# Turning v to channel-major by DMA transposes instead of TensorE matmuls, from the second group on

## The chip, the cores and the metric

The kernel runs on one core of a Trainium2 chip. The metric is device time in microseconds (us), the median of the runs named with it. A ratio is the mean time of one kernel's fast runs over that of the other kernel's fast runs of the same rounds, so it is not quite the ratio of the medians quoted. Faster or slower takes 2%. Spans in the profiles are about 2 us shorter than device times.

## The reference

```python
B, N, C = (4, 6080, 256)                 # q, k, v: float32
qn = q / (norm(q, axis=1) + 1e-06);  kn = k / (norm(k, axis=1) + 1e-06)
s = kn.transpose(0, 2, 1) @ qn / tau     # 256 x 256 for each of 4 batches
a = softmax(s)
x = (v @ a).reshape(24320, 256)
h = x @ w_in                             # 256 -> 2048
g = s * relu(h) ** 2 + b
out = g @ w_out                          # 2048 -> 256
```

## The kernel before

The kernel never forms `v @ a`: it folds the softmax into the first weight (`wa`) and computes `h` from v itself. For this v must lie with channels on the partitions (`vT`), while it arrives with rows on the partitions, so each block of v is transposed; the text calls this the turn of v. The rows are cut into 48 groups of 512 (the last has 256), each group into 16 steps. A step is two matmuls into `h_ps` (L417), ReLU on Scalar, a square on Vector, and, four to five steps later, four matmuls into `o_ps` (L441). At the end of a group Vector copies `o_ps` out of PSUM into `o_sb` (the eviction) and adds `rowconst`, a row made once from sums over w_out. Side work (loads, turns of v, the Gram matrix of the next batch) is hung on steps.

```python
def load_v(g):                      # GpSimd queue, float32 to fp16
    ...
    v16 = vpool.tile([P, TG // P, C], FP16, tag="v16", name="v16")      # 4 buffers
    po(nc.gpsimd.dma_start(out=v16[:, :nj, :], in_=...))

def transpose_v(g):
    _, nj = group(g)
    v16 = v_tiles.pop(g)
    vT_ps = ps_h.tile([P, CH, TG], FP16, tag="h_ps", name="vT_ps")
    for j in range(nj):
        for ch in range(CH):
            po(nc.tensor.transpose(vT_ps[:, ch, ts(j, P)], v16[:, j, ts(ch, P)], ident16))   # L272
    vT = vtpool.tile([P, CH, TG], FP16, tag="vT", name="vT")            # 3 buffers
    po(nc.vector.tensor_copy(out=vT[:, :, : nj * P], in_=vT_ps[:, :, : nj * P]))             # L274
    vT_tiles[g] = vT
...
for c in range(len(g0.chunks)):     # start: all q and k of batch 0, then
    g0.load(c)
# w_in, v of group 0, w_out in two halves, v of groups 1 and 2, in this order on GpSimd's queue
...
at_step((g - 3) * FT + 2, lambda g=g: load_v(g))          # g >= 3, FT = 16 steps
at_step((g - 1) * FT + 4, lambda g=g: transpose_v(g))     # g >= 1; used from step 16 g on
```

## Time and profile before

Device time before is 783.38 us (783.3 to 783.8, three runs).

| | busy us | share of the span |
|---|---|---|
| TensorE (PE) | 753.2 | 96% |
| Scalar (ACT) | 517.8 | 66% |
| Vector (DVE) | 505.2 | 65% |
| GpSimd (POOL) | 57.2 | 7% |

The prediction below shows the page's chain and the groups concerned. A row of a group reads: line, engine, operation, output and input, count, then busy us and mean ns, then idle time of the engine before it and what ended that.

### The profile page before, as it was taken

To read this page: it belongs to the slowest core of one execution; us is meant where nothing else is said; L and a number is where in the kernel's file an instruction comes from. 1 tells how busy PE (TensorE), PEld (TensorE's weight loads), DVE (VectorE), ACT (ScalarE), POOL (GpSimd) and SP (SyncE) were. 2 spreads that over 40 slices of the span, in tenths; PEclk is the share of its full clock that TensorE was granted. 3 is DMA by queue.
4 is the path that set the end of the run, shared out by engine and by line. 5 is a ranking of instruction groups with operands and counts; after the bars stand their busy time and mean duration, and the time that the engine had idled before them with its cause. 6 is when DMAs were issued, how large, how long until landed. Compare 5 with 4: busy or idle time off the path is not lost.

```text
span 781.2 us, 14420 instructions
## 1 busy us (share of the span) xinstructions
PE 753.2 (96%) x5646; PEld 527.4 (68%) x5646; DVE 505.2 (65%) x1106; ACT 517.8 (66%) x858; POOL 57.2 (7%) x111
## 2 busy tenths in 40 slices
PE   2689999999999999999999999999999999999997
PEld 2456777767677777776667667776667766666666
DVE  3767676676656766666566666766566565565565
ACT  3466666666766666766766666666676666666665
POOL 3410010001000010000001000000000000000000
PEclk9689999999999999999999999999999999999999
DMA  8999425115535164124715645131113113121011
GB/s 158 212 263 186 96 44 130 41 41 101 131 76 115 41 133 95 41 42 85 145 41 96 129 85 108 46 75 45 41 48 74 42 42 83 42 52 51 28 55 42
DMA packets 22421, 66.34 MB, mean 85 GB/s; under 512 B 2752, under 2 KB 3328, under 8 KB 22352
## 3 DMA queue, kind: packets, MB, share of 16 engines
q0 software_dynamic: 15152, 40.51, 29.4%
q1 hardware_dynamic: 7200, 24.91, 9.8%
q8 instruction: 44, 0.72, 0.4%
q14 instruction: 25, 0.20, 0.1%
HBM read 78.91 MB, written 24.90 MB: 133 GB/s over the span
## 4 chain that ended last, share of the span: by engine, by line
PE 93%; DMA 5%; issue 1%; ACT 1%; DVE 0%; POOL 0%; POOLq 0%
PE o_ps L441 42%; PE h_ps L417 42%; PE s_ps L120 4%; DMA qc<-in_q_dram 4%; PE vT_ps L272 3%; PE wa_ps L237 2%; DMA v<-in_v_dram 1%; ACT r L420 0%; PE n_ps L185 0%; ACT eT L214 0%; PE t_ps L208 0%; ACT L214 0%; DVE o_sb L449 0%; PE rc_ps L338 0%; POOL kc L108 0%
## 5 line engine op out<-in xcount | busy, mean ns | idle before, releaser
L420 ACT ACTIVATE r<-h_ps 128x512 f16<-128x512 f32 (+1 forms) x768 | 450.0, 593 | 225.8 <-PE h_ps L417 199.9
L427 DVE TENSOR_TENSOR g<-r 128x512 f16<-128x512 f16 (+1 forms) x768 | 321.9, 420 | 243.4 <-ACT r L420 236.6
L441 PE MATMUL o_ps<-w_out,g 128*128 128x256 f16 x3040 | 456.8, 273 | 0.0
L417 PE MATMUL h_ps<-vT,wa 128*128 128x512 f16 (+7 forms) x1632 | 453.0, 364 | 0.6 <-ACT r L420 0.6
L441 PEld LDWEIGHTS <-g 128*128 128x128 f16 x3040 | 295.2, 98 | 183.0 <-DVE g L427 0.2
L417 PEld LDWEIGHTS <-wa 128*128 128x128 f16 x1632 | 157.9, 98 | 30.0 <-issue 0.8
L120 PE MATMUL s_ps<-qc,kc 128*128 128x256 f16 (+1 forms) x384 | 72.9, 296 | 18.5 <-DMA qc<-in_q_dram 18.5
L449 DVE SCALAR_TENSOR_TENSOR o_sb<-o_ps,s_out,rowconst 128x512 f32<-128x512 f32 x95 | 71.1, 748 | 6.4 <-PE o_ps L441 5.6
L261 POOL DMA_DIRECT2D v<-in_v_dram x48 | 25.7, 535 | 617.0 <-PE vT_ps L272 597.6
L143 ACT ACTIVATE sq<-kc 128x1024 f16<-128x1024 f16 (+3 forms) x49 | 50.0, 1031 | 21.9 <-DMA kc<-in_k_dram 18.7
L120 PEld LDWEIGHTS <-kc 128*128 128x128 f16 (+1 forms) x384 | 40.2, 106 | 26.8 <-issue 10.2
L140 DVE TENSOR_TENSOR sq<-qc 128x1024 f16<-128x1024 f16 (+3 forms) x49 | 32.6, 675 | 11.1 <-DMA qc<-in_q_dram 11.1
L274 DVE COPY vT<-vT_ps 128x1024 f16<-128x1024 f16 (+1 forms) x48 | 32.5, 677 | 4.3 <-PE vT_ps L272 4.3
L156 DVE TENSOR_TENSOR f<-sq 128x1024 f16<-128x1024 f16 (+1 forms) x47 | 31.8, 685 | 0.3
L272 PE MATMUL vT_ps<-ident,v 128*128 128x128 f16 x380 | 29.5, 221 | 2.0 <-DMA v<-in_v_dram 2.0
L272 PEld LDWEIGHTS <-v 128*128 128x128 f16 x380 | 25.5, 99 | 3.5 <-DMA v<-in_v_dram 2.4
L156 DVE TENSOR_TENSOR f<-f 128x512 f16<-128x512 f16 (+3 forms) x47 | 25.8, 550 | 0.4
L237 PE MATMUL wa_ps<-w_in,eT 128*128 128x512 f16 x64 | 18.9, 398 | 0.0
L242 ACT ACTIVATE wa<-wa_ps,rs 128x512 f16<-128x512 f32 x16 | 11.0, 687 | 7.6 <-PE wa_ps L237 4.3
L108 POOL DMA_DIRECT2D qc<-in_q_dram x26 | 14.2, 548 | 13.7 <-DMA qc<-in_q_dram 7.7
L108 POOL DMA_DIRECT2D kc<-in_k_dram x26 | 14.2, 548 | 11.4 <-DMA kc<-in_k_dram 9.1
L244 DVE TENSOR_SCALAR wa<-wa_ps,rs 128x512 f16<-128x512 f32 x16 | 11.9, 745 | 1.4 <-PE wa_ps L237 1.2
(37 smaller groups left out, 55.9 us busy)
## 6 DMA issues: line engine op xcount, KB each, us to landing
out_dram<-o_sb SPq DMA_DIRECT2D x47, 512.0 KB, 3.7
v<-in_v_dram POOLq DMA_DIRECT2D x47, 256.0 KB, 5.1
kc<-in_k_dram POOLq DMA_DIRECT2D x20, 512.0 KB, 8.1
qc<-in_q_dram POOLq DMA_DIRECT2D x20, 512.0 KB, 10.0
w_out<-in_moe_w_out_dram POOLq DMA_DIRECT2D x2, 1024.0 KB, 13.2
kc<-in_k_dram POOLq DMA_DIRECT2D x3, 480.0 KB, 8.4
qc<-in_q_dram POOLq DMA_DIRECT2D x3, 480.0 KB, 10.3
w_in<-in_moe_w_in_dram POOLq DMA_DIRECT2D x1, 1024.0 KB, 12.5
```

Source lines behind the costliest of these rows:

```text
L120: po(nc.tensor.matmul(self.s_ps[:, ch, :], kc[:np_, j, ts(ch, P)], qc[:np_, j, :], start=(c == 0 and j == 0 and ch == 0), stop=(c == len(s ...
L140: po(nc.vector.tensor_mul(st["sq"][:np_, 0, js, :], qc[:np_, js, :], qc[:np_, js, :]))
L143: po(nc.scalar.activation(out=st["sq"][:np_, 1, js, :], in_=kc[:np_, js, :], func=AF.Square))
L156: po(nc.vector.tensor_add(st["f", half][:np_, arrays], src[:np_, arrays, :half, :], src[:np_, arrays, half : 2 * half, :]))
L237: po(nc.tensor.matmul(wa_ps, st["e"][:, j, ts(m, P)], w_in16[:, j, ds(fo * NW, NW)], start=(j == 0), stop=(j == CH - 1)))
L272: po(nc.tensor.transpose(vT_ps[:, ch, ts(j, P)], v16[:, j, ts(ch, P)], ident16))
L274: po(nc.vector.tensor_copy(out=vT[:, :, : nj * P], in_=vT_ps[:, :, : nj * P]))
L417: po(nc.tensor.matmul(dst, wa[:, ci, ts(m, P)], src, start=(ci == 0), stop=(ci == CH - 1), skip_group_check=True))
L420: po(nc.scalar.activation(out=r16[:, :n], in_=h_ps[:, :n], func=AF.Relu))
L427: po(nc.vector.tensor_mul(g16[:, :n], r16[:, :n], r16[:, :n]))
L441: po(nc.tensor.matmul(o_halves[g, h][:, j % 2, :], g16[:, ts(j, P)], w_out16[:, m, :], start=(m == 0 and j == js[0]), stop=(m == FT - 1 an ...
L449: po(nc.vector.scalar_tensor_tensor(out=o_sb[:, js[0] : js[-1] + 1, :], in0=o_halves.pop((g, h)), scalar=s_out, op0=ALU.mult, in1=rowconst ...
```

## The change

The intent is to take the turn of v off TensorE, which bounds the kernel. From group 1 on, four DMA transposes per group on the SP queue take the place of eight matmuls and a copy. (The DMA's transposing path is called the crossbar below.) They are placed early (26 steps ahead of use, except for groups 1 and 2 at the start), the loads of v a group earlier, and v and vT get one more buffer each.

```diff
-    vpool = ctx.enter_context(tc.tile_pool(name="vpool", bufs=4))
-    vtpool = ctx.enter_context(tc.tile_pool(name="vtpool", bufs=3))
+    vpool = ctx.enter_context(tc.tile_pool(name="vpool", bufs=5))
+    vtpool = ctx.enter_context(tc.tile_pool(name="vtpool", bufs=4))
...
+    def crossbar_v(g):
+        _, nj = group(g)
+        v16 = v_tiles.pop(g)
+        vT = vtpool.tile([P, CH, TG], FP16, tag="vT", name="vT")
+        for j in range(nj):
+            po(nc.sync.dma_start_transpose(out=vT[:, :, ts(j, P)], in_=v16[:, j, :]))
+        vT_tiles[g] = vT
...
         if g >= 3:
-            at_step((g - 3) * FT + 2, lambda g=g: load_v(g))
+            at_step(max(g - 4, 0) * FT + 2, lambda g=g: load_v(g))
         if g >= 1:
-            at_step((g - 1) * FT + 4, lambda g=g: transpose_v(g))
+            at_step(max((g - 2) * FT, 4 * (g - 1)) + 6, lambda g=g: crossbar_v(g))
```

## The prediction

> **What bounds the kernel now.** I read the page first (busy shares, then the chain that ended last, then the groups), next the waits, next the timeline around one turn of v, and last the start-up. The busy shares and the chain:
>
> ```profile
> PE 753.2 (96%) x5646; PEld 527.4 (68%) x5646; DVE 505.2 (65%) x1106; ACT 517.8 (66%) x858; POOL 57.2 (7%) x111
> ...
> PE 93%; DMA 5%; issue 1%; ACT 1%; DVE 0%; POOL 0%; POOLq 0%
> PE o_ps L441 42%; PE h_ps L417 42%; PE s_ps L120 4%; DMA qc<-in_q_dram 4%; PE vT_ps L272 3%; PE wa_ps L237 2%; DMA v<-in_v_dram 1%; ACT r L420 0%; PE n_ps L185 0%; ACT eT L214 0%; PE t_ps L208 0%; ACT L214 0%; DVE o_sb L449 0%; PE rc_ps L338 0%; POOL kc L108 0%
> ```
>
> A busy share of 96% alone proves little, since matmuls overlap in the records. The chain is the stronger view: 93% of the span is TensorE work that nothing but the matmul before it releases, and the turn of v (vT_ps, L272) is 3% of the span inside that chain. Vector, Scalar and GpSimd together carry about 1%. So TensorE's own stream of rows sets the end, and the turn of v lies in it. The groups concerned:
>
> ```profile
> L274 DVE COPY vT<-vT_ps 128x1024 f16<-128x1024 f16 (+1 forms) x48 | 32.5, 677 | 4.3 <-PE vT_ps L272 4.3
> ...
> L272 PE MATMUL vT_ps<-ident,v 128*128 128x128 f16 x380 | 29.5, 221 | 2.0 <-DMA v<-in_v_dram 2.0
> ```
>
> The mean of 221 ns is not what a turn costs the path, because eight of them run pipelined. The cost is the distance between the starts on either side, in the timeline of TensorE:
>
> ```profile
> 410.94 0.60 PE L417 MATMUL h_ps<-vT,wa 128*128 128x384 f16 x4
> 411.38 0.60 PE L441 MATMUL o_ps<-w_out,g 128*128 128x256 f16 x4
> 411.81 0.60 PE L417 MATMUL h_ps<-vT,wa 128*128 128x384 f16 x4
> 412.25 0.60 PE L441 MATMUL o_ps<-w_out,g 128*128 128x256 f16 x4
> 412.69 0.61 PE L272 MATMUL vT_ps<-ident,v 128*128 128x128 f16 x8
> 413.13 0.60 PE L417 MATMUL h_ps<-vT,wa 128*128 128x384 f16 x4
> ```
>
> A step without the turn is 411.81 - 410.94 = 0.87 us; the step with it is 413.13 - 411.81 = 1.32 us. The difference, 0.44 to 0.45 us, is the distance from 412.69 to 413.13: eight turns at 55 ns. I read the same 0.44 to 0.45 us at 256, 600, 614, 700 and 715 us. There is no gap on either side, so the copy on Vector costs TensorE nothing: vT is made twelve steps before it is used.
>
> **What the Trainium skill says.** (1) "TensorE: Matmul & The Clock Gate", Part 4, gives about 390 ns for one 128x128 turn alone and about 275 ns in one kernel. The trace disagrees for the cost on the path: 55 ns. I use the trace. (2) "VectorE: DVE Perf Modes", The three transpose paths, gives 1309 ns for one 128x128 turn by the DMA crossbar. No run here shows it yet; I use it as the pessimistic rate. (3) "DMA: Bandwidth & Descriptors", Issuing engines are not separate DMA queues: transfers from all issuers run on the same 16 engines and interleave. The trace before has no transpose on any queue, so it cannot show how one shares them. (4) "Perfetto Trace Analysis", Identifying Dependency Chains, says that an instruction with several waits may have extra semaphore instructions put ahead of it; below I say what the trace shows of their cost.
>
> **The change part by part.**
>
> Removed from TensorE: the turn of groups 1 to 47. L272 ran 380 times; group 0 keeps its eight, so 372 go: 46 full groups of eight and a last one of four. 46 x 0.44 us = 20.2 us, and the last, at 758.08 to 758.30, 0.22 us. Together 20.5 us, all of it on the path: 783.4 - 20.5 = 762.9 us.
>
> Removed from Vector: 47 copies out of PSUM, 47 x 0.68 = 32 us of its 505 busy. Off the path: it makes 0 us. The same for the PSUM buffer that vT_ps took from the pool of four: in the whole trace TensorE waited 0.6 us for Scalar to free one.
>
> Added: four transposes per group on the SP queue, each 128x256 fp16, so two 128x128 blocks and 64 KB. 46 x 4 + 2 = 186 of them, 12 MB in all. Per group at the pessimistic 1.31 us per block, one after another: 8 x 1.31 = 10.5 us (an estimate from the skill's figure). A group lasts about (781 - 47) / 47.5 = 15.5 us now, 15.0 us later, so even that rate keeps up. The SP queue otherwise issues one store of the output per group, 0.33 to 0.35 us of issue (at 67.42 and 413.67). The DMA engines are busy 36 to 47% of 100 to 500 us and 13 to 24% after, and there the transposes have room.
>
> Moved: the transposes of group g are placed at step 16(g-2)+6, behind the store of group g-3 at step 16(g-2)+4, and are needed at step 16g. That is 26 steps x 0.87 = 22.6 us of lead for 10.5 us of work. The loads of v are placed a group earlier and v has a fifth buffer; GpSimd no longer waits for TensorE to turn a group but for the SP queue's transposes to have read it:
>
> ```profile
> POOL v L261 <- PE vT_ps L272: 597.6, 42, 16.0
> ```
>
> Those 597.6 us are GpSimd standing before its next load: idle time of an engine that issues transfers, worth nothing by itself. It says that v buffers pace all its loads, those of q and k behind them too. After the change buffers come free earlier, and all loads run further ahead.
>
> **The tight place is group 1**, which has the least lead:
>
> ```profile
> 34.18 1.12 POOL L261 DMA_DIRECT2D v<-in_v_dram  x2
> ...
> 49.96 0.61 PE L272 MATMUL vT_ps<-ident,v 128*128 128x128 f16 x8
> ...
> 60.04 0.59 PE L417 MATMUL h_ps<-vT,wa 128*128 128x512 f16 x2
> ```
>
> The load of v for group 1 is the first of the pair at 34.18, behind w_out. In the slices of 30 to 70 us the rate is near 410 GB/s from 41 to 46 us, which I take for w_out (no change of type, so twice the rate); v for group 1 then lands near 47.5 us (256 KB at 215 GB/s is 1.2 us after it; my inference). Counting steps of 0.87 us, group 1 is first used at the matmul of 60.04 us. So there are 12 us for an estimated 10.5 us, while the loads already fill the 16 engines. It should just do; if other loads get in between, TensorE waits once for some microseconds. Group 2 follows to about 69 us and is needed after 75. I allow 1 us on average for group 1, which makes 763.8 us.
>
> **The rivals.**
>
> A wait at each group start. The first matmul of a group waits for four transfers instead of one copy, so for several semaphores. Three extra instructions of 50 ns would be 0.15 us x 47 = 7 us and leave 770 us. Against it: L120 waits for two DMA tiles (kc and qc), and its two matmuls at 414.88 are followed by the next at 415.10, just their own 0.22 us. TensorE's queue hides such waits once the data is there. I give it one in ten.
>
> The DMA becomes the bound. If a transpose took a multiple of 1.31 us per block, or held up the loads of q and k beside it, each group would wait for vT: at double the rate, 21 us of transposes per 15 us group, the span would pass 1000 us. The engines' free share and the long lead speak against it; that the trace has no transpose in it leaves it possible. One in twenty-five.
>
> Only the start suffers. Between 36 and 68 us the engines are full. If packets of the transposes alternate with loads and each waits its turn, group 1 could come 5 to 10 us late: 768 to 773 us, within 2%. One in six.
>
> The gain is hidden anyway. If another engine were close behind TensorE, taking 20 us away would only uncover it. Against it: Scalar at 66% and Vector at 65%; per step of 0.87 us Scalar needs 0.60 and Vector 0.42 for the main work, with idle before each. I see nothing that takes over.
>
> **Range and chances.** The centre is 762.9 + 1 = 763.8 us, 2.5% less. The low end, 761.5 us, is the full gain and a little from the freed Vector at the start. The high end, 770 us, is group 1 late by 7 us or a small wait per group. Faster by over 2% means under 767.7 us, 4.8 us above the bare sum: 0.74. Within 2%: 0.22. Slower by over 2%: 0.04.
>
> **What would show it.** Right: vT_ps stands at eight matmuls in all; the step that had the turn lasts 0.87 us; TensorE's idle time from 100 us on stays near nothing; the waits show no vT, or one wait by the first matmul of group 1; the loads of v no longer wait for vT_ps. Wrong: L417 waits for the DMA of vT at every group start, the issue-to-landing time of a transpose exceeds the lead of 22 us, the span between 47 and 110 us is longer than before, or the first matmul of each group starts late although its data has landed. The prediction falls most easily on the transfer time of a transpose under load, which no view of the kernel before contains.

## More of the kernel before

The queue of GpSimd carries all loads, the hardware queue the stores:

```profile
q0 software_dynamic: 15152, 40.51, 29.4%
q1 hardware_dynamic: 7200, 24.91, 9.8%
```

## The result, and the profile after

The changed kernel took 770.05 us (769.07 to 770.35, four runs) against 783.59 us of the kernel before on the same chip; ratio 0.9825, 95% interval 0.9808 to 0.9842. That is 13.5 us less, but within 2%, and 6.3 us above the predicted centre.

From the page after: the busy shares, the chain, and the queues:

```profile
PE 734.9 (96%) x5274; PEld 507.1 (66%) x5274; DVE 479.4 (62%) x1059; ACT 517.7 (67%) x858; POOL 57.3 (7%) x111
...
PE 90%; DMA 7%; issue 1%; ACT 1%; SPq 0%; POOL 0%; DVE 0%; POOLq 0%
...
q0 software_dynamic: 15152, 40.51, 28.5%
q1 hardware_dynamic: 60768, 37.12, 18.1%
...
vT<-v SPq DMA_TRANSPOSE x186, 2.4
```

TensorE has 372 matmuls fewer (5646 - 5274) and is busy 18.3 us less. But the chain now has 7% of DMA where it had 5%, and one of its pieces is new: the transfer of vT, 2%. The hardware queue has 53,568 packets more for 12.2 MB more: 288 packets for each of 186 transposes, mostly of 256 bytes.

**Where did the time go?** The start of Vector's first eviction of each group (`o_sb`, L449 before, L458 after) is a clock that both traces have:

| end of group | before, us | after, us | after is ahead by |
|---|---|---|---|
| 0 | 65.55 | 72.71 | -7.16 |
| 1 | 81.42 | 88.14 | -6.72 |
| 2 | 97.56 | 103.82 | -6.26 |
| 10 | 224.20 | 227.05 | -2.85 |
| 20 | 379.67 | 378.05 | 1.62 |
| 46 | 770.46 | 757.77 | 12.69 |
| 47 | 777.11 | 764.42 | 12.69 |

From group 0 to group 46 the changed kernel gains 19.85 us in 46 groups, 0.43 us a group (0.29 to 0.45 in every full group when the traces are read group by group): the predicted gain, in full. All that is missing was lost before 72.71 us. In the timeline of TensorE after (start, duration, line and work, and in brackets the idle time before it and what ended that):

```profile
60.40 0.60 PE L450 MATMUL o_ps<-w_out,g 128*128 128x256 f16 x4
65.99 1.01 PE L426 MATMUL h_ps<-vT,wa 128*128 128x512 f16 x2 [4.99 <-DMA vT<-v]
66.80 1.06 PE L450 MATMUL o_ps<-w_out,g 128*128 128x256 f16 x4
...
70.21 1.06 PE L426 MATMUL h_ps<-vT,wa 128*128 128x512 f16 x2
71.06 0.74 PE L450 MATMUL o_ps<-w_out,g 128*128 128x256 f16 x4
...
71.86 0.59 PE L426 MATMUL h_ps<-vT,wa 128*128 128x512 f16 x2
72.29 0.60 PE L450 MATMUL o_ps<-w_out,g 128*128 128x256 f16 x4
```

TensorE stands idle for 4.99 us before the first matmul of group 1. Then the same four matmuls take 1.06 us where they took 0.60 before the wait. The stretches of time show why. Their columns are the length, then busy time of TensorE, its weight loads, Vector, Scalar and GpSimd (with counts), the granted TensorE clock, the DMA share and GB/s; after:

```profile
60.00:63.00 3.00, 1.00 (x8) 0.46 (x5) 3.00 (x7) 0.96 (x2) 0.00 (x0) 1.00 1.10 195
63.00:66.00 3.00, 0.01 (x1) 0.04 (x2) 0.46 (x2) 0.00 (x0) 0.00 (x0) 0.75 1.51 123
66.00:68.00 2.00, 2.00 (x7) 1.25 (x8) 0.33 (x1) 0.60 (x1) 1.59 (x4) 0.50 0.32 48
68.00:70.00 2.00, 2.00 (x8) 0.91 (x6) 0.58 (x2) 0.40 (x1) 1.59 (x4) 0.50 1.05 186
70.00:72.00 2.00, 2.00 (x11) 1.23 (x10) 0.49 (x2) 0.80 (x2) 0.00 (x0) 0.66 1.07 211
72.00:75.00 3.00, 3.00 (x23) 2.06 (x21) 2.53 (x5) 1.75 (x4) 0.00 (x0) 1.00 1.04 206
```

The third number from the right is the clock: 0.75, 0.50, 0.50, 0.66, then 1.00 again. In the kernel before it is 1.00 throughout these stretches. The Trainium skill, "TensorE: Matmul & The Clock Gate", Part 1, says that an idle window of about 3.4 us takes the clock to half, and that as long a stretch of work brings it back. The fall agrees here: TensorE was idle from 61.00 us, and the clock was at 0.50 from about 64.5 us, 3.5 us later. The return took longer than the page's figure: work began again at 65.99 us and the clock was back at about 71.3 us, 5.3 us later.

**Why was group 1 late?** Its transposes were issued from 48.89 us on, 1.25 us each, so issue was over by 54. But the transfers hardly moved. The queues between 54 and 56 us (packets, MB, share of 16 engines), after:

```profile
q0 software_dynamic: 102, 0.40, 97.3%
q1 hardware_dynamic: 100, 0.03, 9.5%
```

and between 64 and 66 us, when the loads had run out:

```profile
q1 hardware_dynamic: 932, 0.21, 142.4%
q0 software_dynamic: 3, 0.00, 1.1%
```

102 packets of loads, 100 packets of transposes: one for one. A packet of a load there is 0.40 MB / 102 = 3.9 KB, one of a transpose about 256 bytes. By the shares of time, a packet of a load held its engine for 0.973 x 2 us x 16 / 102 = 0.31 us, one of a transpose for 0.03 us: taking turns one for one, the transposes got a tenth of the time. The skill has the rule, which the prediction had only as a rival ("If packets of the transposes alternate with loads"): "DMA: Bandwidth & Descriptors", Queues, rings and completion order, says that each engine goes round the queues it has work for, packet by packet. Group 1 is 4 x 288 = 1152 packets; at 100 in 2 us they would need 23 us, for which there were 12. The other stretches from 54 to 62 us read the same (176 and 178, 100 and 99, 102 and 100).

The loss adds up. The first matmul of group 0 starts at 48.91 instead of 47.58 us: 1.33. Of this, 0.46 us is that v of group 0 landed later (L272 at 42.56 against 42.10 us), and 0.86 us that the matmuls of `wa` after it (L237) took 5.53 instead of 4.67 us, on a clock that came back later (experiments 9 and 10). The transposes can't be the cause, since the first was issued at 48.89 us. The wait: 4.99. From the first matmul of group 1 to the end of group 0: 6.72 instead of 5.51 us (65.55 - 60.04 before), 1.21; this holds the cold clock, less a wait of 1.17 us for rowconst that the kernel before had here and that is now over in time (its profile names Scalar, but Vector's last sum for rowconst ended at 62.14 us and the matmul started at 62.24). Together 7.5 us; the table says 7.16 + 0.44 for the turn of group 1 that fell away, 7.6. Group 1 itself is 4.99 + 1.21 = 6.2 us of it.

### The profile page after: what moved, and what is told of

Its sections match the earlier page's. It is cut to its first block, busy times and chain, and to the rows that moved or that the text cites. A ratio compares the mean times of both kernels' runs of the same rounds, so it can differ in the third digit from the quotient of the medians.

```text
span 768.4 us, 14012 instructions
## 1 busy us (share of the span) xinstructions
PE 734.9 (96%) x5274; PEld 507.1 (66%) x5274; DVE 479.4 (62%) x1059; ACT 517.7 (67%) x858; POOL 57.3 (7%) x111
## 2 busy tenths in 40 slices
DMA packets 75988, 78.52 MB, mean 102 GB/s; under 512 B 56320, under 2 KB 56896, under 8 KB 75920
## 4 chain that ended last, share of the span: by engine, by line
PE 90%; DMA 7%; issue 1%; ACT 1%; SPq 0%; POOL 0%; DVE 0%; POOLq 0%
PE o_ps L450 42%; PE h_ps L426 42%; PE s_ps L120 4%; DMA qc<-in_q_dram 4%; DMA v<-in_v_dram 2%; DMA vT<-v 2%; PE wa_ps L237 1%; SPq L283 0%; PE n_ps L185 0%; ACT r L429 0%; ACT eT L214 0%; PE t_ps L208 0%; POOL kc L108 0%; POOL w_out L295 0%; PE rc_ps L347 0%
## 5 line engine op out<-in xcount | busy, mean ns | idle before, releaser
L426 PEld LDWEIGHTS <-wa 128*128 128x128 f16 x1632 | 159.6, 98 | 36.2 <-issue 6.3
L120 PE MATMUL s_ps<-qc,kc 128*128 128x256 f16 (+1 forms) x384 | 71.8, 291 | 19.3 <-DMA qc<-in_q_dram 19.2
L458 DVE SCALAR_TENSOR_TENSOR o_sb<-o_ps,s_out,rowconst 128x512 f32<-128x512 f32 x95 | 71.1, 749 | 6.5 <-PE o_ps L450 5.7
L237 PE MATMUL wa_ps<-w_in,eT 128*128 128x512 f16 x64 | 19.8, 415 | 0.0
L237 PEld LDWEIGHTS <-eT 128*128 128x128 f16 x64 | 6.6, 105 | 3.7 <-issue 2.5
L343 DVE TENSOR_TENSOR w_out<-w_out 128x512 f32<-128x512 f32 (+1 forms) x8 | 5.2, 651 | 0.0
```

Of the source, the lines that this page charges most:

```text
L120: po(nc.tensor.matmul(self.s_ps[:, ch, :], kc[:np_, j, ts(ch, P)], qc[:np_, j, :], start=(c == 0 and j == 0 and ch == 0), stop=(c == len(s ...
L237: po(nc.tensor.matmul(wa_ps, st["e"][:, j, ts(m, P)], w_in16[:, j, ds(fo * NW, NW)], start=(j == 0), stop=(j == CH - 1)))
L426: po(nc.tensor.matmul(dst, wa[:, ci, ts(m, P)], src, start=(ci == 0), stop=(ci == CH - 1), skip_group_check=True))
L458: po(nc.vector.scalar_tensor_tensor(out=o_sb[:, js[0] : js[-1] + 1, :], in0=o_halves.pop((g, h)), scalar=s_out, op0=ALU.mult, in1=rowconst ...
```

## The experiments

All changes are to the changed kernel unless said otherwise. Runs of one job share the runs of the kernel before (783.44 us in the first job, 784.12 in the second, 783.98 in the third).

**1. Group 1 back on TensorE.**

```diff
-        if g >= 1:
+        if g == 1:
+            at_step(4, lambda: transpose_v(1))
+        if g >= 2:
```

> Only group 1 goes back to TensorE, at its old place (step 4); groups 2 to 47 stay on the crossbar. Theory (the loss is one late start: 5.0 us of wait for group 1 and a cold TensorE clock for some 5 us after it): the wait by L426 on the transposes is gone, the clock stays at 1.00 between 60 and 75 us, and the time is 762.9 + 0.44 for group 1 = 763.3 us, up to 764.7 if the 1.3 us later start of the first matmul stays. Rival (the loss is spread: a cost at each group start, or other transfers held up by transposes): at most 0.5 us better than the changed kernel, so about 769.5 us.

Measured: 764.5 us (763.88 to 764.85), ratio 0.9755. No wait for vT is left in the trace, and the clock is 1.00 from 60 to 75 us:

```profile
63.00:66.00 3.00, 2.62 (x17) 1.86 (x18) 1.52 (x4) 1.19 (x2) 0.00 (x0) 1.00 1.11 188
66.00:68.00 2.00, 2.00 (x16) 1.37 (x14) 1.73 (x4) 1.19 (x2) 0.00 (x0) 1.00 1.07 207
```

So one group of 47 cost 5.5 us. The rival of a loss spread over the groups falls. This kernel is still 1.15 us behind the kernel before at the end of group 0; experiment 9 is about that.

**2. Loads and buffers alone.** All turns back on TensorE at their old steps; fifth v buffer, fourth vT buffer and early loads stay.

```diff
-            at_step(max((g - 2) * FT, 4 * (g - 1)) + 6, lambda g=g: crossbar_v(g))
+            at_step((g - 1) * FT + 4, lambda g=g: transpose_v(g))
```

> All turns back on TensorE with their copies, at their old steps; only the fifth v buffer, the fourth vT buffer and the earlier loads of v are kept. Theory (buffers and early loads are worth nothing by themselves): 783.5 us, within 0.5 us of before. Rival (the earlier loads of v, which come ahead of q and k at the start, delay the first matmul): about 1.3 us more than before, 784.9 us.

Measured: 783.77 us, ratio 1.0004 (0.9988 to 1.0021). The loads and buffers by themselves do nothing, good or bad; and the first matmul is not delayed by them (0.09 us ahead of before at the end of group 0).

**3. One transpose per group instead of four.**

```diff
-        for j in range(nj):
-            po(nc.sync.dma_start_transpose(out=vT[:, :, ts(j, P)], in_=v16[:, j, :]))
+        po(nc.sync.dma_start_transpose(
+            out=vT[:, :nj].rearrange("p j c q -> p (j c) q"),
+            in_=v16[:, :nj, :].rearrange("p j c -> p (j c)")))
```

> One transpose of 128x1024 per group instead of four of 128x256; vT is laid out with the block number outside. Theory A (each transpose costs a fixed price for setup and completion, so four of them are slow beside full loads): group 1 lands several microseconds earlier, the 5.0 us wait goes to under 2 us, about 764 to 767 us. Theory B (the price is per 256-byte packet: the changed kernel added 288 packets a transpose, and each waits its turn among the packets of the loads): the packets are as many, group 1 is as late, 769 to 771 us.

Measured: 770.01 us, ratio 0.9827; TensorE waits 4.7 us for group 1 as before. Between 54 and 56 us the queues show 101 packets of loads and 101 of transposes. Theory A falls, and the counts fit theory B: the price is per packet, and one instruction of 256 KB has nearly as many packets as four of 64 KB.

**4. A quiet start.** The loads that compete with group 1 are held on GpSimd until step 9, and the next batch's first stage starts later so that its loads are not missed.

```diff
+    def hold_pool():
+        po(nc.gpsimd.tensor_copy(out=gate, in_=g16s[9][:, 0:1]))
+    at_step(9, hold_pool)
+    at_step(9, lambda: load_v(2))             # was loaded before the first step
-            at_step(max(g - 4, 0) * FT + 2, lambda g=g: load_v(g))
+            at_step(max((g - 4) * FT + 2, 9), lambda g=g: load_v(g))
-        w0 = first_group[b - 1] * FT + (18 if b == 1 else 6)
+        w0 = first_group[b - 1] * FT + (40 if b == 1 else 6)
-            at_step(max(3, sc - 16), ...gr.load(c))
+            at_step(max(10, sc - 16), ...gr.load(c))
```

> All of groups 1 to 47 on the crossbar as in the changed kernel, but the loads of v from group 2 on and those of the next batch's q and k are held on GpSimd until step 9 (about 57 us), and that batch's first stage starts 22 steps later; so the engines carry nothing else while group 1 is transposed. Theory (the transposes of group 1 are slow only because loads fill the 16 engines): four issues of about 1.24 us, landing by about 57 us, no wait for group 1, 763 to 765 us unless the held loads come late themselves. Rival (the first transposes are slow by themselves, or the wait comes from the late landing of v): the wait of 4 to 5 us stays, 769 to 771 us.

Measured: 766.11 us, ratio 0.9778. Between 48 and 54 us the four transposes of group 1 land 2.4 us after their issue, where they took 13.2 us in the changed kernel in the same stretch. First this kernel, then the changed one:

```profile
q1 hardware_dynamic: 864, 0.20, 16.8%
q0 software_dynamic: 15, 0.02, 1.6%
...
vT<-v SPq DMA_TRANSPOSE x4, 2.4
```

```profile
q0 software_dynamic: 526, 1.26, 108.6%
q1 hardware_dynamic: 76, 0.02, 2.3%
...
vT<-v SPq DMA_TRANSPOSE x4, 13.2
```

Group 1 is in time. The held loads themselves then made a later group late by 2.25 us (at 79.10 us, the transposes landing 10 to 13 us after issue among the loads released), which accounts for the time above the 765 us expected. It is the same mechanism at another place: the loads, not the crossbar by itself and not the issue, set the landing.

**5. The old buffers.** On top of experiment 1: four v buffers, three vT buffers, loads of v at their old steps.

```diff
-    vpool ... bufs=5            ->   bufs=4
-    vtpool ... bufs=4           ->   bufs=3
-            at_step(max(g - 4, 0) * FT + 2, lambda g=g: load_v(g))
+            at_step((g - 3) * FT + 2, lambda g=g: load_v(g))
```

> The kernel with group 1 on TensorE (764.5 us), with the buffers and loads of v of the kernel before: four v buffers, three vT buffers, loads a group later. Theory (the late group 1 came from the full engines at the start, and later groups have 22 us of lead): no wait for vT appears, 764.5 us within 0.7. Rival (the crossbar's longer hold on the v buffers is what the fifth buffer pays for): loads of v come late, transposes of some groups land after their step, waits by L428 on vT, over 766 us.

Measured: 764.17 us (763.03 to 765.14), ratio 0.9742; no wait for vT. The fifth buffer and the early loads are not needed.

**6. Twice as many transposes.** On top of experiment 1, every group from 8 on is transposed a second time into a tile that nobody reads.

```diff
+        if g >= 8:
+            vX = vtpool.tile([P, CH, TG], FP16, tag="vX", name="vX")
+            for j in range(nj):
+                po(nc.sync.dma_start_transpose(out=vX[:, :, ts(j, P)], in_=v16[:, j, :]))
```

> The kernel with group 1 on TensorE (764.5 us), and every group from 8 on is transposed a second time into a tile that nothing reads: 158 more transposes. Theory (in the steady state the transposes are hidden wholly and do not slow TensorE): 764.5 us within 0.7; SP then issues for some 10 us of the 14 us of a group. Rival (transposes cost TensorE or the loads something each): double that cost, at least 1 us slower; if the second set makes SP or the crossbar the bound, waits by L428 on vT.

Measured: 764.83 us, ratio 0.9752 against 0.9755 of experiment 1. The DMA share from 100 to 400 us rises from 0.45 in experiment 1 to 0.61, the median landing over the whole run from 2.4 to 3.5 us, and TensorE sees nothing of it. In the steady state the transposes are hidden, with room for as many again.

**7. Keeping the clock up during the wait.** Group 1 is late as in the changed kernel, but 16 matmuls into an unused PSUM tile stand where TensorE would be idle.

```diff
+        if s == FT:
+            warm_ps = ps_h.tile([P, TG], FP32, tag="h_ps", name="warm_ps")
+            for _ in range(16):
+                po(nc.tensor.matmul(warm_ps, w_in16[:, 0, :P], w_in16[:, 0, :TG], ...))
```

> The changed kernel (group 1 still late) with 16 matmuls of 128x512 into an unused PSUM tile just before the first matmul of group 1, where TensorE stands idle for 5.0 us: 3.5 us of work that nobody needs. Theory (the wait is paid twice, by its own 5 us and by some 2.4 us more at half clock after it): the clock stays at 1.00 from 60 to 72 us and the time falls by 1.5 to 2.5 us to about 767.5 to 768.5 us. Rival (only the wait counts; the slow steps after it have another cause): 770 us, no change.

Measured: 767.0 us (766.85 to 767.79), ratio 0.9783, half a microsecond better than the best that was expected. The clock is 1.00 from 60 to 75 us. Its timeline:

```profile
60.44 3.62 PE L420 MATMUL warm_ps<-w_in 128*128 128x512 f16 x16
65.40 0.59 PE L431 MATMUL h_ps<-vT,wa 128*128 128x512 f16 x2 [1.35 <-DMA vT<-v]
65.83 0.60 PE L455 MATMUL o_ps<-w_out,g 128*128 128x256 f16 x4
```

The data come as late as ever, yet useless work in the gap makes the kernel 3 us faster: the steps after the wait run at full speed. At the end of group 0 it is 3.2 us ahead of the changed kernel; 0.6 of that is that its transposes landed sooner (65.40 against 65.99 us), so the cold clock is worth some 2.6 us, a little more than expected.

**8. More lead for group 1.** The load of v for group 1 goes ahead of the two loads of w_out.

```diff
     load_v(0)
+    load_v(1)
     w_out_rows = ...
     ...
-    load_v(1)
     load_v(2)
```

> The changed kernel with the load of v for group 1 moved ahead of the two loads of w_out. Theory (group 1 only lacks lead: it took 17 us beside full loads and had 12): v for group 1 lands some 5 us sooner, near 43.8 us, its transposes land near 60.5 us or sooner, the wait is 0 to 1 us, the clock stays up, and the time is 763.5 to 765 us; w_out lands 1.2 us later, which may cost up to 0.5 us. Rival (the transposes end when the loads let up, whenever they start): they land near 65 us again, 769 to 770 us.

Measured: 770.75 us, ratio 0.9827, no better. The transposes were issued 5.1 us earlier (from 43.76 us), and group 1 was used later still:

```profile
66.97 1.01 PE L426 MATMUL h_ps<-vT,wa 128*128 128x512 f16 x2 [5.45 <-DMA vT<-v]
```

My theory missed here and the rival fits: as long as the loads fill the engines, an earlier issue gains little. From 48 to 62 us the packets alternate again (109 and 109, 104 and 103 in two of the 2 us stretches). The packet count alone would have had group 1 through near 63 us; the traces show what held its last transfer. The last load then under way, of q, was issued at 49.51 us and landed 17.1 us later, at 66.6; the last transpose of group 1, issued at 47.65, landed 19.2 us later, at 66.8. In the changed kernel the two landed at 65.2 (49.40 + 15.8) and 65.9 us (52.78 + 13.1). So in both the transposes end just after the loads do. The loads end because no new ones come: GpSimd's next load of v waits for these transposes to free a buffer (17.4 us here, 16.5 in the changed kernel). Why that load of q ended 1.4 us later here is open.

**9 and 10. Keeping the clock up before the first group.** 48 matmuls of 128x128 on a tile of ones, while TensorE waits for the load of v for group 0; once on top of experiment 1, once in the kernel before.

```diff
+    warm_ps = ps_h.tile([P, P], FP32, tag="h_ps", name="warm_ps")
+    for _ in range(48):
+        po(nc.tensor.matmul(warm_ps, ones16, ones16, start=True, stop=True, ...))
     transpose_v(0)
```

> The kernel with group 1 on TensorE (764.5 and 764.2 us in two jobs) with 48 matmuls of 128x128 on a tile of ones, which nobody reads, between 39.8 and 42.5 us, where TensorE waits for the load of v for group 0. Theory (what is still missing against the bare sum, 1.15 to 1.5 us at the end of group 0, is a TensorE clock that stays at half from 42 to some 47 us, while in the kernel before it came up at some 45 us): the clock is 1.00 from 42 us on or soon after, the first matmul of group 0 starts 1 to 2 us sooner than 48.8 us, and the time is 762 to 763.3 us. Rival (the later start comes from loads that land later): no change, 764.2 to 764.5 us.

> The kernel before with the same 48 matmuls at the same place. Theory: there the clock comes up at about 45 us, so the gain is smaller, 0.5 to 1.2 us, about 782.5 us. Rival (no effect of the clock): 783.5 us.

Measured: 762.4 us (ratio 0.9732, the fastest of all) and 783.18 us (ratio 0.9993, interval 0.9979 to 1.0007). Of the four runs on top of experiment 1 three took 762.01 to 762.46 and the profiled one 764.31; in that one the clock had gone to 0.51 between 40 and 42 us in spite of the matmuls, and its mean over the run was 0.991, against 0.996 to 0.998 in the three. In the profile of the kernel before with them the clock stays at 1.00 from 36 to 50 us, and it is 1.22 us ahead at the end of group 0; but its runs spread from 781.75 to 784.56: the two with a mean clock of 0.995 took 781.75 and 781.91, the three with 0.991 to 0.993 took 783.18 to 784.56. So a clock that stays up at the start is worth 1 to 2 us in the runs that have it, and whether it does differs from run to run; as a median it brings nothing clear to the kernel before.

The kernels with transposes and no matmuls here all start their first group 0.9 to 1.9 us late in their profiles (48.50 to 49.43 against 47.58 us). The clock falls in all of them and in the kernel before too, but there and in experiment 2 it is back by about 45.3 us, in the others between 46.5 and 48.5, and the first matmul follows in nearly the same order. Why it is back later in these, and why v of group 0 landed 0.46 us later in the changed kernel, is not settled.

## Why the prediction was right or wrong

- **What bounds the kernel: right.** TensorE's stream sets the end before and after.
- **The turn costs 0.44 us a group and all of it comes back: right.** 19.85 us came back from group 0 to group 46, and 0.44 for group 1 before; the sum said 20.5. No other engine took over.
- **Copy, buffers, loads of v worth nothing: right.** Experiments 2 and 5.
- **No price at the start of each group for waiting on four transfers: right.** A price of 0.15 us a group would have shown in the table. (The 50 ns of that rival was an assumption; no run measured it.)
- **The steady state hides the transposes: right.** One lands 2.4 us after issue in the median; even twice as many cost nothing. The sum of 1.31 us per block was too high there: on quiet queues the four transposes of a group took 6.2 us (experiment 4, 49.27 to 55.5), not 10.5.
- **The tight place is group 1: right in place, wrong in size.** The step that failed is "I allow 1 us on average for group 1". That term came to 6.2 us in the traces, and experiment 1 gets 5.5 us back. Two things were left out. The 10.5 us for four transposes took no account of the loads beside them; there they took 17 us (48.89 to 65.99), because 256-byte packets take turns with packets of 3.9 KB. And the wait was counted once: the cold clock after it adds 2.6 us by experiment 7. I also put the landing of v at 47.5 us; the first issue was at 48.89. ("Between 36 and 68 us the engines are full" holds to 66 us; from 66 to 68 the kernel before shows a DMA share of 0.53. Nothing hangs on it.)
- **The later start of group 0, 1.33 us, had no term at all.** It is not the transposes' doing, and its cause is open in part.
- **The range.** The rival "Only the start suffers", at one in six, gave the mechanism and 768 to 773 us, and this is what came: 770.05 us, 0.05 us beyond the upper end of the stated range of 761.5 to 770.0 us, and in the class given 0.22. That end was drawn for "group 1 late by 7 us", so that the range reaches so far is not luck; the centre was carried by the allowance that failed.

## What to carry to other kernels

Before moving work from the bound engine to the DMA, ask what the queues carry in the stretch where the first transfer is due. Here a transfer of many small packets took turns with large ones (100 for 102), so its time beside them went by the number of packets and by how long the large ones last, not by its bytes. Leave the first group on the old path, where the lead is short and the loads are full (5.5 us here), and move those with lead. Count a long wait on TensorE more than once: 4.99 us of idleness brought the clock to half and cost some 2.6 us more, while waits of 1.35 us (experiment 7) and 2.25 us (experiment 4) left it at 1.00.

## What the Trainium skill lacked or had wrong

- "DMA: Bandwidth & Descriptors", DMA Transpose (X-bar): it lacks the packets of a transpose from SBUF. Here a 128x256 fp16 transpose is 288 packets, mostly of 256 bytes, and one of 128x1024 does not have larger ones (51,872 packets under 512 bytes in experiment 3's trace, 56,320 in the changed kernel's).
- "Advanced Engine Details and Errata", X-Bar Transpose (TRN2), has transposes as fast as other DMAs. Here that holds on landing for one transpose of 256 KB (3.7 us in the median in experiment 3, against 3.8 us for a load of v, listed with the same 256 KB, in the changed kernel). It lacks two things: the issue (1.24 us of SP for 64 KB, 1.47 us for 256 KB, where a plain store of 512 KB took 0.34), and the company (beside full loads the landing of 64 KB went from 2.4 to 13 us).
- "VectorE: DVE Perf Modes", The three transpose paths: 1309 ns per 128x128 block is near the 2.4 us of the two blocks of one transpose on quiet queues, but it can't be multiplied: eight blocks in one transpose landed 3.7 us after issue (experiment 3), not 10.5.
- "TensorE: Matmul & The Clock Gate", Part 4: 275 to 390 ns for a turn on TensorE; it lacks what a row of them costs: on the path eight in a row cost 55 ns each here.
- "TensorE: Matmul & The Clock Gate", Part 1: about 3.4 us of work to bring the clock back; here it took 5.3 us (65.99 to 71.3), while the fall after 3.5 us agrees.
